# Hashed attention and a feed-forward block: the second feed-forward product as seven block products, in a remade order

## The chip, the cores and the metric

The kernel runs on one core of a Trainium2 chip. The metric is the device time of one execution in microseconds (us), the median of three runs. A core has five engines that run at the same time and meet only at semaphores: TensorE (PE, matrix products, with weight loads shown as PEld), VectorE (DVE), ScalarE (ACT), GpSimd (POOL) and SyncE (SP, which here issues transfers). Matrix products land in PSUM, which has eight banks of 512 f32 numbers for each of 128 partitions.

## The reference, cut to what matters

```python
# q, k, v: (4, 8, 768, 64); proj: (64, 6); w_ch1: (512, 2048); w_ch2: (2048, 512)
mask = bucket(q @ proj)[..., :, None] == bucket(k @ proj)[..., None, :]    # bucket: the signs as bits
scores = where(mask, q @ k.T / 8, -1e9)
x = softmax(scores) @ v               # then heads side by side: (4, 768, 512)
xn = (x - mean(x)) / sqrt(var(x) + 1e-6) * g_ln
out = x + maximum(xn @ w_ch1, 0.0) @ w_ch2
```

## The kernel before

The 4 x 768 rows are cut into twelve units `u` of 256 rows, three for each of the four batches. A unit goes through attention and then through the feed-forward block, and different units overlap.

Attention works on twice 4 heads (`g`) and on three blocks of 256 keys (`kp`), which makes 72 steps `s`. `S_` (L516) makes the scores: for each of 4 heads and two halves of the keys three matmuls of 256 columns, one of the hash bits (`G`) and two of the q and k halves. `E_` (L522) is the exponential on ScalarE, two instructions a step. `A_` (L541) multiplies by the values, with a column of ones for the sum. Then on VectorE `na` (L554) takes the accumulator out, `nb` (L561, L563) divides by the sum and writes `x`, `nc` (L567) and `ce` (L570, L571) make the statistics and the scaled rows `xc`, and `fl` turns them by a transfer into `xnT`. `rs` on GpSimd makes the reciprocal deviation, which is applied at the very end.

The feed-forward block of a unit: `F_` (L598) makes the first product, 16 blocks of 128 hidden columns for 256 rows, in eight parts `p` of two blocks; `R_` takes each part through max(., 0) into `hb`, on VectorE (L608) or ScalarE (L606). `hb` holds the hidden layer with the hidden column on the partition: 16 blocks `nt`, each 256 rows wide. `D_` (L614) makes the second product: for each half of the rows (`t`), 16 matmuls that sum over `nt`, each with 128 columns of `hb` as weights and 512 columns of `w2_sb` streamed, into one bank `f2`. `Z_` (L622) multiplies by the deviation and adds to `x`; `O_` sends `x` out. In unit 11 the second half of the rows is split into 384 and 128 columns.

Beside this, q and k of the next batch are loaded (`LX`), turned in 32 x 32 blocks on VectorE (`tu`, L270), cast to bf16 (`CA`) and hashed (`hm`, L471); v is cast on GpSimd (`cv`, L417) and summed over the keys there (`su`, L425 to L427). The first batch goes through shorter steps of its own (`lx`, `tn`, `ca`, `ha` at L359, `bh`).

The order is written out by hand or by a planner in the string `ORDER`: each word is a step, an engine letter (v, a, p, s, t) and its numbers, and the program issues the words one after the other. Each engine takes its own words in that order and waits only for the data and buffers it needs. `SLOTS` says which buffer each tile of a kind takes. PSUM is divided by name: `scA`, `scB` and `acc` are two banks each, `f1` and `f2` one each; F uses `f1` (and `f2` in unit 0), D uses `f2`.

Of the kernel before, what the change touches and what calls it, by code (L numbers as in the profile page):

```python
# [9 lines left out]
BF16 = mybir.dt.bfloat16  # L10
AOP = mybir.AluOpType
# [4 lines left out]
ROT = (0, 1, 2)  # L16


ORDER = """
mem.v lp.a lx.a.0.1.0.1 tab.a pf.v lx.s.0.0.0.1 warm.t wm.t.0 wm.t.1 wm.t.2 wm.t.3 sel.p  # L20
tn.v.0.0.0 p32.p tn.v.0.1.0 ca.p.0.1.0 lx.s.0.1.1.3 ha.t.0.0.0 wm.t.4 lx.s.1.1.0.3 lx.s.1.0.0.1 ha.t.0.1.0 lv.s.0.0.4 ca.a.0.0.0
lx.s.0.0.1.3 bh.v.0.0.0 wm.t.5 tn.v.0.1.1 ha.t.0.1.1 lw2.p.1 bh.v.0.1.0 ca.p.0.1.1 S.t.0.2 lv.s.0.4.4 E.a.0.0 E.a.0.1
tn.v.0.1.2 tn.v.1.1.1 ca.p.1.1.1 lx.s.1.0.1.3 wm.t.6 wm.t.7 bh.v.0.1.1 ha.t.1.1.1 on.p.0 bh.v.1.1.1 tn.v.1.1.0 S.t.1.2
E.a.1.0 ca.v.0.1.2 gx.p.1.0.0 ha.t.0.1.2 bh.v.0.1.2 E.a.1.1 tn.v.1.0.0 ca.p.1.0.0 ca.v.1.1.0 ha.t.1.1.0 bh.v.1.1.0 tn.v.1.1.2
S.t.2.2 E.a.2.0 cv.p.0.0.0 ha.t.1.0.0 bh.v.1.0.0 S.t.4.2 cv.p.0.0.2 tn.v.0.0.1 hc.t.0.0.1 ca.p.0.0.1 lw1.p.3 bc.v.0.0.1
gx.p.1.0.1 ha.t.1.1.2 LX.s.1.0.0 tn.v.0.0.2 E.a.2.1 E.a.4.0 LX.s.1.0.1 E.a.4.1 bh.v.1.1.2 sl.t.0.0.1 bi.v.0.0.1 cv.p.0.4.2
A.t.0.2 S.t.3.2 A.t.1.2 ca.v.1.1.2 lg.s lw1.p.1 sq.t.0.0 E.a.3.0 A.t.2.2 sc.v.0.0 E.a.3.1 S.t.5.2
E.a.5.0 cv.p.0.4.0 sq.t.0.4 na.v.0.0 nb.v.0.0 lw1.p.2 lw1.p.0 nc.v.0.0 E.a.5.1 S.t.8.2 sc.a.0.4 A.t.5.2
E.a.8.0 E.a.8.1 tu.v.1.0.0.2 lw2.p.0 tn.v.1.0.1 A.t.4.2 ca.p.1.0.1 hc.t.0.0.2 tn.v.1.0.2 A.t.3.2 tu.v.1.0.1.0 bc.v.0.0.2
lw2.p.3 gx.p.1.1.1 tu.v.1.0.0.1 sl.t.0.0.2 na.v.0.1 bi.a.0.0.2 S.t.6.2 E.a.6.0 LX.s.1.1.1 E.a.6.1 hc.t.1.0.1 nb.v.0.1  # L30
hc.t.1.0.2 bc.v.1.0.2 sl.t.1.0.2 bi.a.1.0.2 bc.v.1.0.1 pmem.p S.t.7.2 A.t.8.2 E.a.7.0 lv.s.1.4.1 nc.v.0.1 ce.v.0.1
ce.v.0.0 ft.t.0.1 lv.s.1.4.2 E.a.7.1 fc.a.0.1 sl.t.1.0.1 tu.v.1.0.1.1 bi.v.1.0.1 A.t.6.2 ft.t.0.0 S.t.9.2 E.a.9.0
on.p.1 lw2.p.2 fc.v.0.0 E.a.9.1 F.t.0.6 F.t.0.7 tu.v.1.0.1.2 R.a.0.6 A.t.7.2 tu.v.1.0.0.0 S.t.10.2 R.v.0.7
na.v.1.0 nb.v.1.0 lv.s.1.4.0 tu.v.1.0.0.3 tu.v.1.0.1.3 E.a.10.0 CA.p.1.0.1 F.t.0.3 F.t.0.4 E.a.10.1 A.t.9.2 ca.a.0.0.2
R.v.0.4 ca.a.1.0.2 S.t.11.2 gx.p.1.1.0 LX.s.1.1.0 E.a.11.0 E.a.11.1 lv.s.1.0.0 hm.t.1.0 R.v.0.3 F.t.0.5 S.t.14.2
R.a.0.5 A.t.11.2 A.t.10.2 E.a.14.0 E.a.14.1 bt.v.1.0 na.v.1.1 nb.v.1.1 F.t.0.2 R.a.0.2 S.t.12.2 nc.v.1.0
E.a.12.1 E.a.12.0 lv.s.1.0.1 F.t.0.0 R.v.0.0 mw.s.1.0 F.t.0.1 R.a.0.1 CA.p.1.0.0 tu.v.1.1.1.0 A.t.14.2 nc.v.1.1
ce.v.1.0 S.t.13.2 E.a.13.0 D.t.0.0.0 lv.s.1.0.3 tu.v.1.1.1.2 lv.s.1.4.3 D.t.0.0.1 fl.s.1.0 tu.v.1.1.0.2 ce.v.1.1 fl.s.1.1
tu.v.1.1.0.0 A.t.12.2 E.a.13.1 LX.s.2.0.0 S.t.16.2 E.a.16.0 E.a.16.1 A.t.13.2 tu.v.1.1.1.3 tu.v.1.1.0.1 tu.v.1.1.0.3 rs.p.0
D.t.0.0.2 D.t.0.0.3 mr.s.1.0.1 cv.p.1.4.0 Z.v.0.0 tu.v.1.1.1.1 CA.p.1.1.1 cv.p.1.4.2 S.t.15.2 lv.s.1.0.2 cv.p.1.0.0 E.a.15.0  # L40
mr.s.1.0.2 mr.s.1.0.3 hm.t.1.1 E.a.15.1 D.t.0.1.0 CA.a.1.1.0 S.t.17.2 E.a.17.1 mr.s.1.0.0 bt.v.1.1 mw.s.1.1 mr.s.1.1.3
na.v.2.0 nb.v.2.0 F.t.1.2 R.v.1.2 su.p.1.0 A.t.15.2 E.a.17.0 cv.p.1.0.2 A.t.16.2 F.t.1.6 S.t.18.2 R.a.1.6
nc.v.2.0 F.t.1.5 R.v.1.5 D.t.0.1.1 mr.s.1.1.2 E.a.18.0 A.t.17.2 E.a.18.1 sp.t.1.0 sc.v.1.0 na.v.2.1 S.t.20.2
E.a.20.0 mr.s.1.1.0 lv.s.2.4.1 F.t.1.0 tu.v.2.0.0.0 R.v.1.0 D.t.0.1.2 F.t.1.4 nb.v.2.1 nc.v.2.1 E.a.20.1 tu.v.2.0.0.3
R.a.1.4 S.t.19.2 E.a.19.0 E.a.19.1 D.t.0.1.3 ce.v.2.0 F.t.1.1 LX.s.2.0.1 su.p.1.4 rs.p.1 R.a.1.1 mr.s.1.1.1
Z.v.0.1 lv.s.2.0.1 lv.s.2.4.3 O.s.0.1 tu.v.2.0.1.2 lv.s.2.0.2 A.t.20.2 tu.v.2.0.1.1 S.t.21.2 ce.v.2.1 E.a.21.0 fl.s.2.0
F.t.1.3 D.t.1.0.0 E.a.21.1 A.t.18.2 rs.p.2 S.t.22.2 R.v.1.3 tu.v.2.0.0.1 tu.v.2.0.0.2 CA.v.2.0.0 A.t.19.2 fl.s.2.1
F.t.1.7 na.v.3.0 tu.v.2.0.1.3 O.s.0.2 R.v.1.7 E.a.22.0 E.a.22.1 D.t.1.0.1 S.t.23.2 F.t.2.1 lv.s.2.4.0 D.t.1.0.2
R.v.2.1 LX.s.3.1.0 nb.v.3.0 E.a.23.0 A.t.22.2 E.a.23.1 lv.s.2.0.0 F.t.2.0 LX.s.2.1.1 D.t.1.0.3 R.a.2.0 tu.v.2.0.1.0
CA.p.2.0.1 hm.t.2.0 S.t.24.2 E.a.24.1 Z.v.1.0 nc.v.3.0 bt.v.2.0 mw.s.2.0 sp.t.1.4 sc.v.1.4 A.t.21.2 lv.s.2.0.3  # L50
mr.s.2.0.2 D.t.1.1.0 A.t.23.2 O.s.0.0 E.a.24.0 na.v.3.1 O.s.0.3 tu.v.2.1.1.0 F.t.2.3 mr.s.2.0.3 cv.p.2.0.0 tu.v.2.1.1.1
R.a.2.3 nb.v.3.1 S.t.26.2 LX.s.2.1.0 D.t.1.1.1 E.a.26.0 E.a.26.1 nc.v.3.1 F.t.2.2 R.v.2.2 ce.v.3.1 D.t.1.1.2
mr.s.2.0.1 S.t.25.2 ce.v.3.0 F.t.2.4 LX.s.3.0.1 A.t.24.2 E.a.25.0 D.t.1.1.3 cv.p.2.0.2 R.v.2.4 S.t.29.2 E.a.25.1
tu.v.2.1.1.2 fl.s.3.1 Z.v.1.1 E.a.29.0 A.t.25.2 E.a.29.1 D.t.2.0.0 fl.s.3.0 F.t.2.7 R.a.2.7 S.t.28.2 A.t.26.2
tu.v.2.1.0.3 F.t.2.5 D.t.2.0.1 E.a.28.0 R.v.2.5 tu.v.2.1.0.1 E.a.28.1 na.v.4.0 S.t.31.2 E.a.31.1 tu.v.2.1.1.3 F.t.3.6
R.v.3.6 A.t.29.2 D.t.2.0.2 tu.v.2.1.0.2 tu.v.2.1.0.0 CA.v.2.1.0 E.a.31.0 F.t.2.6 R.a.2.6 O.s.1.3 S.t.27.2 E.a.27.0
D.t.2.0.3 nb.v.4.0 LX.s.3.0.0 O.s.1.2 hm.t.2.1 LX.s.3.1.1 nc.v.4.0 bt.v.2.1 mw.s.2.1 mr.s.2.1.3 Z.v.2.0 tu.v.3.0.0.2
E.a.27.1 tu.v.3.0.0.1 S.t.30.2 E.a.30.0 rs.p.3 su.p.2.0 F.t.3.4 A.t.27.2 R.a.3.4 on.p.2 D.t.2.1.0 D.t.2.1.1
E.a.30.1 F.t.3.1 R.v.3.1 S.t.32.2 CA.a.2.1.1 O.s.1.1 E.a.32.0 D.t.2.1.2 lv.s.3.0.0 F.t.3.2 tu.v.3.0.1.0 R.v.3.2
O.s.1.0 A.t.28.2 E.a.32.1 lv.s.2.4.2 S.t.35.2 E.a.35.0 E.a.35.1 na.v.4.1 F.t.3.0 cv.p.2.4.0 mr.s.2.0.0 D.t.2.1.3  # L60
Z.v.2.1 O.s.2.0 A.t.30.2 R.a.3.0 O.s.2.1 S.t.34.2 lv.s.3.0.2 mr.s.2.1.2 F.t.3.3 A.t.31.2 E.a.34.0 nb.v.4.1
R.v.3.3 tu.v.3.0.1.1 nc.v.4.1 ce.v.4.1 D.t.3.0.0 fl.s.4.1 ce.v.4.0 fl.s.4.0 E.a.34.1 tu.v.3.0.1.2 S.t.33.2 rs.p.4
D.t.3.0.1 A.t.32.2 E.a.33.0 tu.v.3.0.0.3 E.a.33.1 F.t.3.5 R.a.3.5 S.t.37.2 E.a.37.1 tu.v.3.0.0.0 cv.p.2.4.2 na.v.5.0
nb.v.5.0 D.t.3.0.2 A.t.33.2 F.t.3.7 A.t.35.2 E.a.37.0 R.v.3.7 nc.v.5.0 S.t.38.2 E.a.38.0 D.t.3.0.3 Z.v.3.0
mr.s.2.1.1 F.t.4.3 A.t.34.2 O.s.2.2 na.v.5.1 E.a.38.1 R.a.4.3 lv.s.3.0.3 O.s.2.3 tu.v.3.0.1.3 S.t.36.2 E.a.36.1
CA.v.3.0.1 F.t.4.0 R.a.4.0 nb.v.5.1 mr.s.2.1.0 CA.v.3.0.0 D.t.3.1.0 hm.t.3.0 bt.v.3.0 E.a.36.0 S.t.39.2 mw.s.3.0
E.a.39.0 F.t.4.2 A.t.38.2 R.a.4.2 tu.v.3.1.1.3 E.a.39.1 A.t.37.2 F.t.4.5 R.a.4.5 S.t.40.2 sp.t.2.0 sc.v.2.0
E.a.40.1 D.t.3.1.1 F.t.4.7 E.a.40.0 R.a.4.7 D.t.3.1.2 tu.v.3.1.0.0 S.t.41.2 E.a.41.0 F.t.4.4 R.a.4.4 A.t.36.2
mr.s.3.0.3 nc.v.5.1 ce.v.5.0 fl.s.5.0 ce.v.5.1 rs.p.5 na.v.6.0 su.p.2.4 fl.s.5.1 tu.v.3.1.1.0 D.t.3.1.3 Z.v.3.1
E.a.41.1 lv.s.3.0.1 F.t.4.1 R.v.4.1 S.t.44.2 E.a.44.0 E.a.44.1 A.t.41.2 D.t.4.0.0 F.t.5.2 S.t.43.2 E.a.43.0  # L70
tu.v.3.1.1.1 on.p.3 nb.v.6.0 A.t.40.2 nc.v.6.0 R.v.5.2 F.t.4.6 D.t.4.0.1 E.a.43.1 S.t.42.2 R.v.4.6 F.t.5.3
D.t.4.0.2 E.a.42.1 tu.v.3.1.0.2 cv.p.3.0.0 R.v.5.3 A.t.39.2 sp.t.2.4 E.a.42.0 O.s.3.3 sc.v.2.4 na.v.6.1 nb.v.6.1
S.t.45.2 E.a.45.1 E.a.45.0 lv.s.3.4.3 D.t.4.0.3 O.s.3.0 A.t.44.2 F.t.5.5 R.a.5.5 tu.v.3.1.1.2 A.t.43.2 S.t.47.2
E.a.47.0 Z.v.4.0 F.t.5.7 nc.v.6.1 ce.v.6.1 mr.s.3.0.1 O.s.3.1 E.a.47.1 fl.s.6.1 A.t.42.2 O.s.3.2 ce.v.6.0
na.v.7.0 D.t.4.1.0 S.t.46.2 E.a.46.0 D.t.4.1.1 lv.s.3.4.0 A.t.47.2 R.v.5.7 F.t.5.1 E.a.46.1 tu.v.3.1.0.1 A.t.45.2
# [605 lines left out]
```

## Time and profile before

| What | Value |
|---|---|
| Median of three runs | 305.0 us (304.3 to 305.05) |
| Span of the profiled execution, first to last instruction | 302.0 us |
| Mean granted TensorE clock | 1.000 |
| PE busy | 290.5 us (96%) |
| DVE busy | 175.9 us (58%) |
| ACT busy | 189.0 us (63%) |
| POOL busy | 76.4 us (25%) |
| Matmuls recorded, weight loads recorded | 4345, 4394 |

The time of the profiled execution itself is not listed apart from the runs; its span is 3.0 us under their median, and what is worked out on the span is carried over with these 3.0 us. The shares are means over the whole span. Each matmul has one weight load, so 49 records of matmuls are missing; they are all among those of L614 (351 of 400), and a group of L614 can therefore show fewer than its four matmuls. The end of a matmul in the records is modelled, so the time that one takes in a stream is read from start to start. In a group's row the last numbers are the idle time of its engine just before it and what ended that.

### The profile page before, as it was taken

What the parts mean: (1) busy time and instruction counts of PE and PEld (TensorE: products, weight loads), DVE (VectorE), ACT (ScalarE), POOL (GpSimd) and SP (SyncE); (2) the same over time, 40 slices, a digit from 0 to 9 for tenths busy, and PEclk for the clock granted to TensorE, in tenths of its full rate; (3) what the DMA queues carried; (4) which work ended last, traced back from release to release, by engine and by line L of the source; (5) the groups of instructions that cost most, each with busy time, mean ns of one, the idle gap of its engine ahead of it and who ended that gap; (6) DMA issues with size and microseconds to landing.
All of it is one profiled execution on the core that took longest, in us unless ns stands there. A gap on an engine that the chain in (4) does not pass through costs nothing.

```text
span 302.0 us, 9823 instructions
## 1 busy us (share of the span) xinstructions
PE 290.5 (96%) x4345; PEld 202.5 (67%) x4394; DVE 175.9 (58%) x364; ACT 189.0 (63%) x206; POOL 76.4 (25%) x103
## 2 busy tenths in 40 slices
PE   8988899999999999999999999999999999999995
PEld 4666677676766767677666776667666776676663
DVE  4878758759767564875749466274554346443322
ACT  2587888778646777777667866854565665643010
POOL 5497062476017101300750002700101001001000
PEclk9999999999999999999999999999999999999999
DMA  6999999718768453420322242012201501003132
GB/s 221 310 299 247 282 212 270 177 35 230 201 159 246 84 217 95 98 72 18 80 66 41 68 100 51 21 35 54 54 2 35 106 2 37 20 2 89 52 87 71
DMA packets 31194, 34.32 MB, mean 114 GB/s; under 512 B 15536, under 2 KB 27824, under 8 KB 31152
## 3 DMA queue, kind: packets, MB, share of 16 engines
q1 hardware_dynamic: 26080, 28.98, 35.0%
q0 software_dynamic: 4224, 4.19, 8.5%
q8 instruction: 34, 0.56, 0.8%
q10 hardware_dynamic: 848, 0.53, 0.7%
q14 instruction: 8, 0.07, 0.1%
HBM read 28.12 MB, written 6.88 MB: 116 GB/s over the span
## 4 chain that ended last, share of the span: by engine, by line
PE 94%; ACT 3%; issue 1%; DVE 0%
PE f L598 29%; PE sc L516 19%; PE acc L541 12%; PE hp L471 3%; ACT E L522 3%; PE hf L359 2%; PE warm L328 1%; PE f_110None L614 1%; PE f_101None L614 1%; PE f L614 1%; PE f_90None L614 1%; PE f_20None L614 1%; PE f_80None L614 1%; PE f_21None L614 1%; PE f_00None L614 1%
## 5 line engine op out<-in xcount | busy, mean ns | idle before, releaser
L522 ACT ACTIVATE E<-sc,bias_sb 128x1024 bf16<-128x1024 f32 x144 | 153.5, 1111 | 60.6 <-PE sc L516 60.6
L598 PE MATMUL f<-xnT,w_sb 128*128 128x256 bf16 x768 | 99.3, 273 | 0.1
L598 PEld LDWEIGHTS <-w_sb 128*128 128x128 bf16 x768 | 70.8, 98 | 22.6 <-issue 7.4
L608 DVE TENSOR_SCALAR hb<-f 128x512 bf16<-128x512 f32 x49 | 33.7, 690 | 59.2 <-PE f L598 58.8
L614 PEld LDWEIGHTS <-hb 128*128 128x128 bf16 x400 | 36.0, 98 | 31.2 <-issue 3.0
L516 PE MATMUL sc<-qb,kb 32*128 32x256 bf16 x1152 | 52.4, 267 | 0.0
L606 ACT ACTIVATE hb<-f 128x512 bf16<-128x512 f32 x47 | 28.0, 596 | 35.9 <-PE f L598 35.9
L541 PEld LDWEIGHTS <-E 128*128 128x128 bf16 x1152 | 42.7, 98 | 8.2 <-issue 3.2
L541 PE MATMUL acc<-vaug,E 128*128 128x65 bf16 x1152 | 46.2, 194 | 0.1
L516 PE MATMUL sc<-G 6*128 6x256 bf16 (+1 forms) x576 | 42.6, 273 | 2.7 <-ACT E L522 2.0
L576 POOL TENSOR_SCALAR rs<-mv 128x2 f32<-128x2 f32 x12 | 7.7, 640 | 106.9 <-DVE mv L570 106.6
L516 PEld LDWEIGHTS <-kb 32*128 32x128 bf16 x1152 | 30.4, 93 | 1.5
L516 PEld LDWEIGHTS <-G 6*128 6x128 bf16 (+1 forms) x576 | 15.7, 91 | 20.7 <-issue 17.4
L417 POOL CAST vaug<-vn 128x768 bf16<-128x768 f32 x16 | 14.0, 884 | 58.3 <-DMA vn<-in_v_dram 44.2
L270 DVE STREAM_TRANSPOSE T<-X 128x384 f32<-128x384 f32 (+2 forms) x52 | 26.8, 542 | 1.2 <-DMA X<-in_k_dram 1.2
L554 DVE SCALAR_TENSOR_TENSOR y<-vsB,acc 128x520 f32<-128x520 f32 x24 | 16.5, 688 | 10.5 <-PE acc L541 10.2
L571 DVE SCALAR_TENSOR_TENSOR xc<-x,mv,gB 128x512 bf16<-128x512 f32 x24 | 18.6, 775 | 0.9
L567 DVE BATCH_NORM_STATS2 st<-x 128x6 f32<-128x256 f32 x48 | 17.7, 412 | 0.3
L563 DVE TENSOR_TENSOR x<-y,rc 128x512 f32<-128x512 f32 x24 | 16.8, 699 | 0.8
L425 POOL TENSOR_TENSOR t<-vn 128x768 f32<-128x768 f32 x6 | 10.9, 1812 | 0.0
L281 POOL CAST kb<-T 128x1536 bf16<-128x1536 f32 x3 | 4.4, 1461 | 22.3 <-DVE T L270 22.3
L270 DVE STREAM_TRANSPOSE tp<-X 128x256 f32<-128x256 f32 x24 | 9.0, 416 | 1.4 <-DMA X<-in_q_dram 0.9
(113 smaller groups left out, 236.7 us busy)
## 6 DMA issues: line engine op xcount, KB each, us to landing
out_dram<-x SPq DMA_DIRECT2D x45, 128.0 KB, 2.0
X<-in_k_dram SPq DMA_DIRECT2D x7, 768.0 KB, 5.8
X<-in_q_dram SPq DMA_DIRECT2D x6, 768.0 KB, 4.7
vn<-in_v_dram SPq DMA_DIRECT2D x24, 192.0 KB, 6.0
w_sb<-in_moe_w_ch_dram POOLq DMA_DIRECT2D x8, 512.0 KB, 15.9
vn<-in_v_dram SPq DMA_DIRECT2D x2, 768.0 KB
X<-in_q_dram SPq DMA_DIRECT2D x2, 512.0 KB, 12.2
Bd<-B SPq DMA_DIRECT2D x6, 96.0 KB, 2.5
```

Source lines behind the costliest of these rows:

```text
L270: nc.vector.transpose(d[:, j], s[:, j, kj0 : kj0 + n])
L516: nc.tensor.matmul(sc(s, i // 2)[:, i % 2, 256 * kk : 256 * kk + 256], lh, rh, start=(rep == 0), stop=(rep == 2), skip_group_check=True,)
L522: nc.scalar.activation(E(s)[:, heads(h)], sc(s, h), AF.Exp, scale=EXP_SCALE, bias=bias_sb)
L541: nc.tensor.matmul(acc[:, qt, (D + 1) * i : (D + 1) * (i + 1)], E(s)[:, i, 256 * kk + P * qt : 256 * kk + P * qt + P], vaug(u // 3)[:, 4 * ...
L554: nc.vector.scalar_tensor_tensor(yt(u, g), vs, EPS_ROW, made[f"acc{u}{g}"][:, :, :A], op0=AOP.mult, op1=AOP.add,)
L563: nc.vector.tensor_tensor(xo, a[:, :, :, 0:D], rc.to_broadcast([P, 2, 4, D]), op=AOP.mult)
L567: nc.vector.bn_stats(stats(u)[:, qt, g], xt(u)[:, qt, 256 * g : 256 * g + 256])
L571: nc.vector.scalar_tensor_tensor(xc(u)[:, t], xt(u)[:, t], mv(u)[:, t, 0:1], gB, op0=AOP.subtract, op1=AOP.mult,)
L598: nc.tensor.matmul(f1[:, n].rearrange("p (t x) -> p t x", t=2), w1_sb[:, dt, P * nt : P * nt + P], xnT(u)[:, :, dt], start=(dt == 0), stop ...
L606: nc.scalar.activation(hb(u)[:, 2 * p : 2 * p + 2], f1, AF.Relu)
L608: eng.tensor_scalar_max(hb(u)[:, 2 * p : 2 * p + 2], f1, 0.0)
L614: nc.tensor.matmul(f2, hb(u)[:, nt, P * t : P * t + P], w2_sb[:, nt, half(h)], start=(nt == 0), stop=(nt == NNT - 1),)
```

## The change

Units 1 to 11 get another second product. The hidden layer of a unit and the second weight matrix are each cut into 2 x 2 blocks, A (rows by hidden columns) and B (hidden columns by output columns), and the product is made of seven block products instead of eight, in Winograd's form:

```
S1 = A21 + A22   S2 = S1 - A11   S3 = A11 - A21   S4 = A12 - S2
T1 = B12 - B11   T2 = T3 + B11   T3 = B22 - B12   T4 = B21 - T2
P1 = A11 B11   P2 = A12 B21   P3 = S4 B22   P4 = A22 T4   P5 = S1 T1   P6 = S2 T2   P7 = S3 T3
C11 = P1 + P2    C12 = P1 + P6 + P5 + P3
C21 = P1 + P6 + P7 + P4    C22 = P1 + P6 + P7 + P5
```

A block product `P` is 8 matmuls of 256 columns. P1, P6, P7 and P4 are added up in one accumulator X, which `Y` reads after each of them; P5 and P3 share one, Yb; P2 has its own. Each `Y` adds a partial sum into a quarter of `x` (128 rows, 256 columns). The four sums of weights are made once, in eight `sw` (half of them on GpSimd); the four sums of a unit, `ss`, are each one instruction over 128 x 1024 bf16, 25 of them on VectorE and 19 on GpSimd, and S3 takes the place of A21 in `hb`. Of the R steps 64 are on ScalarE and 32 on VectorE (47 and 49 before). Unit 0 keeps `D_` and `Z_`. PSUM tiles are dealt from two pools, three pairs of banks `pp` (scores, accumulators of attention) and two banks `f` (all the rest: F, P, D and the hash products), as the strings in `SLOTS` say. `ORDER` and `SLOTS` are remade from beginning to end. In the last stretch F, R, `ss`, `P` and `Y` of unit 11 stand behind each other with no scores left.

```diff
 ORDER (the end of it)
-D.t.11.1.0.0 D.t.11.1.1.0 D.t.11.1.2.0 O.s.8.2 D.t.11.1.3.0 D.t.11.1.0.1 D.t.11.1.1.1 rs.p.11 Z.v.11.0 O.a.11.0.0 O.s.11.0.1 Z.v.11.1.0
...
+R.a.10.3 F.t.10.5 F.t.10.4 O.s.9.3 R.a.10.5 F.t.10.0 R.a.10.4 P.t.10.2 Y.v.10.2 R.a.10.0
+F.t.11.4 ss.v.10.1 O.s.9.2 ss.v.10.2 R.a.11.4 P.t.10.1 Y.v.10.1 ss.v.10.4 P.t.10.5 P.t.10.6
+Y.v.10.5 P.t.10.3 Y.v.10.6 ss.p.10.3 Y.v.10.3 P.t.10.7 Y.v.10.7 F.t.11.0 R.a.11.0 P.t.10.4
...
+F.t.11.3 R.a.11.3 F.t.11.5 R.a.11.5 F.t.11.2 O.s.10.0 R.a.11.2 ss.v.11.1 ss.p.11.3 P.t.11.2
+Y.v.11.2 P.t.11.1 ss.v.11.2 O.s.9.1 Y.v.11.1 ss.v.11.4 P.t.11.5 Y.v.11.5 O.s.10.1 P.t.11.6
+Y.v.11.6 P.t.11.3 Y.v.11.3 O.s.10.2 O.s.11.0.0 O.a.11.0.1 P.t.11.7 Y.v.11.7 O.s.11.1.0.1 Y.v.11.7.1.0
+P.t.11.4 O.a.11.1.1.1 Y.v.11.4 O.a.11.1.1.0 O.s.11.1.0.0
...
+    wt = {n: pool.tile([P, 8, 256], BF16, name=f"wt{n}") for n in (2, 3, 4)}
...
     def ps(name, shape, tag, dt=F32):
         if name not in made:
-            made[name] = psum.tile(shape, dt, name=name, tag=tag)
+            n = taken.get(tag, 0)
+            taken[tag] = n + 1
+            made[name] = psum.tile(shape, dt, name=name, tag=f"{tag}_{SLOTS[tag][n]}")
...
-    def D_(eng, u, t, qtr, h=None):
...
+    def Hq(u, t, kh):
+        return hb(u)[:, 8 * kh : 8 * kh + 8, P * t : P * t + P]
+
+    def Wq(kh, h):
+        return w2_sb[:, 8 * kh : 8 * kh + 8, 256 * h : 256 * h + 256]
+
+    def Ss(u, k):
+        return Hq(u, 1, 0) if k == 3 else sb(f"S{u}{k}", [P, 8, P], BF16, "tp", 3)
...
+    def ss(eng, u, k):
+        out, in0, in1, op = {
+            1: (1, Hq(u, 1, 0), Hq(u, 1, 1), AOP.add),
+            2: (2, None, Hq(u, 0, 0), AOP.subtract),
+            3: (3, Hq(u, 0, 0), Hq(u, 1, 0), AOP.subtract),
+            4: (4, Hq(u, 0, 1), None, AOP.subtract),
+        }[k]
+        in0 = Ss(u, 1) if in0 is None else in0
+        in1 = Ss(u, 2) if in1 is None else in1
+        eng.tensor_tensor(Ss(u, out), in0, in1, op=op)
+
+    def prod(u, k):
+        if k in (1, 6, 7) or (k == 4 and u < NU - 1):
+            return "X"
+        return {2: "Ya", 5: "Yb", 3: "Yb", 4: "Yc"}[k]
+
+    def P_(eng, u, k):
+        left = {1: Hq(u, 0, 0), 2: Hq(u, 0, 1), 4: Hq(u, 1, 1)}
+        lh = left[k] if k in left else Ss(u, {3: 4, 5: 1, 6: 2, 7: 3}[k])
+        rh = {1: Wq(0, 0), 2: Wq(1, 0), 3: Wq(1, 1), 4: wt[4], 5: Wq(0, 1), 6: wt[2], 7: wt[3]}[k]
+        name = f"{prod(u, k)}{u}"
+        first = name not in made
+        f2 = ps(name, [P, 256], "f")
+        for n in range(8):
+            nc.tensor.matmul(f2, lh[:, n], rh[:, n], start=(first and n == 0), stop=(n == 7), skip_group_check=True)
+
+    def Y_(eng, u, k, *more):
+        t, h = more or {1: (0, 0), 2: (0, 0), 3: (0, 1), 4: (1, 0), 5: (1, 1), 6: (0, 1), 7: (1, 1)}[k]
+        x = xt(u)[:, t, 256 * h : 256 * h + 256]
+        nc.vector.scalar_tensor_tensor(
+            x, made[f"{prod(u, k)}{u}"], rstd(u)[:, t : t + 1], x, op0=AOP.mult, op1=AOP.add,
+        )
```

In the changed file `P_` is at L692, `Y_` at L697, `ss` at L677, `R_` at L634 and L636, `F_` at L626.

## The prediction

> **What bounds the kernel now.** The page comes first: its busy times, and the chain that ended last.
>
> ```profile
> span 302.0 us, 9823 instructions
> PE 290.5 (96%) x4345; PEld 202.5 (67%) x4394; DVE 175.9 (58%) x364; ACT 189.0 (63%) x206; POOL 76.4 (25%) x103
> PE 94%; ACT 3%; issue 1%; DVE 0%
> ```
>
> A busy PE need not be a full one, so the second view is the waits of PE alone, longest first:
>
> ```profile
> PE sc L516 <- ACT E L522: 2.0, 4, 0.7
> PE warm L328 <- DVE bias_sb L286: 1.1, 1, 1.1
> PE sc L516 <- DVE G L273: 0.6, 1, 0.6
> PE hf L383 <- DVE Bc L273: 0.5, 1, 0.5
> ```
>
> All of these lie in the first 35 us. After that TensorE has no wait for another engine over 0.1 us: each microsecond of matmul taken out is a microsecond off the span, if nothing new makes TensorE wait. The third view is the timeline of PE near the end, where only feed-forward products are left; it prices a matmul of each width:
>
> ```profile
> 286.66 1.04 PE L598 MATMUL f<-xnT,w_sb 128*128 128x256 bf16 x8
> 287.53 1.03 PE L614 MATMUL f_101None<-w_sb,hb 128*128 128x512 bf16 x4
> 288.39 1.04 PE L598 MATMUL f<-xnT,w_sb 128*128 128x256 bf16 x8
> ```
>
> From start to start, 8 matmuls of 256 columns take 0.87 us (109 ns each) and 4 of 512 take 0.86 (216 ns). So columns set the price, the fixed part is some 2 ns, and a weight load before each narrow matmul is hidden, since L598 has that already.
>
> **What the change saves.** A unit's second product was 32 matmuls of 512 columns: 32 x 0.216 = 6.91 us. Seven block products of 8 matmuls of 256 are 56 x 0.109 = 6.10. Ten units at 0.81 and unit 11 (its split halves summed 0.05 more) give 9.0 us. Unit 0 keeps D. The first score step also stands behind one hash product (L359) fewer, which took 0.96 us before it started at 9.13 us: I take 0.9, with 0 to 1.5 as its bounds, since ScalarE's exps follow closely there. Without new waits the span is 302.0 - 9.0 - 0.9 = 292.1.
>
> The Trainium skill, page "TensorE: Matmul & The Clock Gate", section "Back-to-back issue gap", speaks against the change: it gives 131 ns a matmul for a sustained stream with 512 columns and 81 with 128. By an estimate half-way between, 98 ns for 256, a unit would go from 4.2 to 5.5 us. The trace disagrees (216 and 109 ns).
>
> **What it costs the other engines.** Z at L622 took 0.75, 0.62 and 0.35 us for 512, 384 and 128 columns, so a Y of 256 takes 0.48 by a straight line. Out go the 20 Z of units 1 to 10 and the three of unit 11 (16.7 us), in come 78 Y (37.7). 17 R move from VectorE to ScalarE (-11.7, and +10.1 there). Sums: 29 on VectorE, 23 on GpSimd. No row shows a tensor_tensor all in bf16. L563 takes 0.70 for 512 f32; L591 shows 512 bf16 in the time (423 ns) that L447 needs for 256 f32 (424), so bf16 goes at double rate, and 1024 bf16 cost about 0.70. At L563's own rate they would cost 1.23; I take 0.70. Casts and copies that move to VectorE add 4.2, so it comes to 175.9 - 16.7 + 37.7 - 11.7 + 20.3 + 4.2 = 210 us (225 at 1.23). On GpSimd L425 (768 elements, 1.81 us) and L426 (256, 0.73) give 2.12 ns an element: a sum costs 2.35 us; bounds 1.1 (L417's one-input rate) and 2.7 (the dear L279 cast, 4.08 for 1536). 23 sums and three casts bring it to some 134 us. ScalarE stays at 190, since casts leave it as R comes. None is a bound over the whole span, but counted along ORDER from S.18 to S.42 VectorE has 77 us queued (83 at 1.23) against TensorE's 91, and from S.30 to S.36 it has 23 (25) against 24.
>
> **What makes TensorE wait.** Six of the seven products share two accumulators: P6 may start when Y1 has read bank X, P7 when Y6 has, P4 when Y7 has, P3 when Y5 has; P5, P6, P7, P3 need sums. VectorE takes its queue in order, so each Y stands behind the sums. And there is a contention in the trace of before. Three timelines, of VectorE and GpSimd together and then of each alone:
>
> ```profile
> 180.77 0.82 POOL L417 CAST vaug<-vn 128x768 bf16<-128x768 f32 x1 [25.36 <-DMA vn<-in_v_dram]
> 180.81 1.32 DVE L571 SCALAR_TENSOR_TENSOR xc<-x,mv,gB 128x512 bf16<-128x512 f32 x1
> ```
> ```profile
> 69.12 0.85 DVE L563 TENSOR_TENSOR x<-y,rc 128x512 f32<-128x512 f32 x1
> ```
> ```profile
> 68.70 0.72 POOL L426 TENSOR_TENSOR t<-t 128x256 f32<-128x256 f32 x1
> 69.50 1.06 POOL L427 TENSOR_TENSOR vsum<-t 128x256 bf16<-128x256 f32 x1
> ```
>
> L571 (two tensors from SBUF) takes 0.75 us elsewhere; started just behind a GpSimd cast it took 1.32, that is until the cast was done and its own work after. L563 waited for L426 and then L427 for L563. So a VectorE instruction with two SBUF inputs and a GpSimd one that reads exclude each other for their whole length. Y and na, with one input in PSUM, are free of it: L622 kept its 0.75 beside L425. The Trainium skill, "SBUF — State Buffer", section "Who interferes with whom", says the same of two SBUF inputs, and that whoever issues first gets the ports. By it too, the sums split over both engines block each other; the trace agrees (1.32 us against 0.75).
>
> I walk units through their queues with these prices (a reader of PSUM starts 0.22 us after the matmuls' slot; 0.1 us for a semaphore).
>
> Unit 11, from the end of F.11.2 as zero: R ends 0.8, first sum 0.9 to 1.6, Y2 to 2.1, P2 and P1 and P5 run to 2.6. The second sum would end at 2.8, Y1 at 3.3, so P6 starts 3.4, P3 at 4.6, P4 ends 7.2: 1.1 over the 6.1 of pure work. But ss.p.11.3 is released by the same first sum, while VectorE is in Y2: GpSimd holds the port from 1.7 to 4.05, the second sum ends at 4.6, and all after it is 1.8 later.
>
> Unit 10: both sums run first on VectorE, ss.p.10.3 then holds the port from 3.05 to 5.4, and the third sum waits from 3.55; Y5 and Y6 stand behind it, P3 starts at 6.5 instead of 4.8. By order alone 0.4, by the port 1.7.
>
> Unit 8: as unit 11, with Y2 between the sums: 1.0 and 1.8. Unit 7: ce.8.0 comes while ss.p.7.2 runs, Y1 and so P6 are 1.0 late, over 0.5 by order alone. Unit 6: third sum behind ss.p.6.2, covered by S, F: 0.3 and 0. Unit 9: both GpSimd sums run while VectorE has only Y's: 0 and 0.
>
> Units 6 to 11 lose 3.3 by order and 6.3 by the port. Units 1 to 5 I did not walk; scores and F lie between their products as in 6 and 7, so I give each those units' mean, 0.4 and 0.5: 2.0 and 2.5. In unit 2, ss.p.2.4 and ss.v.2.3 with nb.4.1 behind it meet, so it may be more. Total: 5.3 by order, 8.8 by the port. If the sums cost 1.23, each unit's chain of two to three is up to 1 us longer (some 4 more where not covered); with GpSimd sums at 1.1 the port costs 4 instead of 8.8. The order alone has as bounds 2.5 (half, where engines run ahead) and 8.
>
> Sum: 292.1 + 5.3 + 8.8 = 306.2 of span. The median of the runs, 305.0, lies 3.0 above the profiled span of 302.0, and I add the same: 309.
>
> **Rivals.** (1) The port is not met on the path: the order places the GpSimd sums where VectorE is in Y's, transposes or R's, as it does in unit 9. For it: 7 such meetings in the trace of before, over 41 GpSimd reads, and none made TensorE wait. Against: in units 7, 8, 10 and 11 the same instruction releases both sides. It gives 292.1 + 5.3 + 3.0 = 300.4 us, faster. The change wins as soon as the port costs less than 3.7, two of the four meetings. Chance 0.40 for this side.
> (2) VectorE becomes the bound in units 2 to 5: its 77 us of 91 grow by five or six blocked instructions of up to 2.35, so Y's and R's run late throughout and F waits for its two banks too. For it: its queue is over 80% full there; against: R left it. It adds 3 to 5 to the forecast: 312 to 314. Chance 0.10.
> (3) Matmuls are paid by the piece: if a narrow matmul cost over 124 ns (6.91/56), the products would save nothing. The rows give 109 and the fixed part 2 ns. At 130 ns, 56 x 21 ns x 11 = 13 us more than the sum: 322. Chance 0.02. This is what the skill's rule on the gap would amount to; the trace speaks against it.
> That the products are not there is no rival: the instruction list has 616 matmuls of 256 columns where 368 stood.
>
> **Numbers.** About 0.3%, 0.9 us, is what a measurement of this kernel can tell from no change. Forecast (order and port) 0.41, own range 306 to 314; VectorE bound 0.10; by the piece 0.02; port not met 0.40, own range 297.5 to 303.5; in between, 304.1 to 305.9, 0.07. So faster 0.40, same 0.07, slower 0.53. The range goes from 298 (rival 1 with the order's waits at half, 2.5: 292.1 + 2.5 + 3.0 = 297.6) to 314; some 0.08 is left out below it and 0.10 above.
>
> **What would show it.** Right: Matmul groups of the products at 109 ns; PE's waits, new, on VectorE's Y (L697) and sums (L677), 10 us or more together, most in units 7, 8, 10, 11; VectorE's sums of 0.70 that last 2 to 3 us whenever a GpSimd sum runs; PE busy under 285. Wrong: sums on both engines overlapping at full speed, or PE waits under 6 us in total, which would give a time under 302; or idle PE before E or F, which would put the cost elsewhere.

## The result and the profile after

The changed kernel takes 318.6 us (median of four runs, 315.9 to 320.4) against 304.7 us for the kernel before: a ratio of 1.046, with an interval of 1.040 to 1.051. It is 14 us slower; the forecast was 309, with 314 as the upper end. Ratios leave out executions that took over 1.5% more than the fastest of the same kernel (five of ten in run 6, at most a third in any other); in runs 6, 13 and 16 the ratio is therefore given and not the median.

The profiled execution took 318.7 us, 1.7 more than its span. Its page, first the length, the busy times and the chain that ended last:

```profile
span 317.0 us, 10500 instructions
...
PE 290.3 (92%) x4642; PEld 228.3 (72%) x4642; DVE 228.2 (72%) x438; ACT 190.5 (60%) x213; POOL 131.8 (42%) x129
...
PE 54%; DVE 18%; DMA 13%; issue 5%; SPq 3%; POOL 3%; ACT 3%; DVEq 0%; POOLq 0%
```

The chain had been 94% PE. Now 18% of it is VectorE and 13% transfers, where the kernel before had next to nothing of either. The waits of PE, longest in total first (us in total, times, longest):

```profile
PE X L692 <- DVE x L697: 6.0, 6, 1.7
PE Yb L692 <- DVE x L697: 3.7, 4, 2.2
PE f L626 <- DMA w_sb<-in_moe_w_ch_dram: 2.8, 1, 2.8
PE sc L544 <- DMA G<-Bd: 1.6, 1, 1.6
PE f L641 <- DVE B L302: 1.3, 1, 1.3
```

The first two rows, 9.7 us, are the new waits of products on Y that were forecast. Their place was not: 5.4 of them lie in units 1 to 3, 0.3 in unit 4, and 4.0 in units 7, 8, 10 and 11, where most were expected. The next two rows are a weight transfer and the hash bits, which the prediction did not have. All gaps of PE come to 21.1 us, against 6.6 before.

The products themselves cost what was said. The timeline of PE near the end:

```profile
309.70 1.03 PE L692 MATMUL Yb<-w_sb,S 128*128 128x256 bf16 x8
310.57 1.04 PE L692 MATMUL X<-wt,hb 128*128 128x256 bf16 x8
311.44 1.04 PE L692 MATMUL Yc<-wt,hb 128*128 128x256 bf16 x8
```

A group of eight starts every 0.87 us, 109 ns a matmul. And the meeting of the two engines in unit 11 came as walked. VectorE's timeline, then GpSimd's:

```profile
304.82 0.69 DVE L677 TENSOR_TENSOR S<-hb 128x1024 bf16<-128x1024 bf16 x1 [5.38 <-ACT hb L634]
305.43 0.48 DVE L697 SCALAR_TENSOR_TENSOR x<-Ya,rs,x 128x256 f32<-128x256 f32 x1
305.82 2.43 DVE L677 TENSOR_TENSOR S<-S,hb 128x1024 bf16<-128x1024 bf16 x1
```
```profile
305.59 2.12 POOL L677 TENSOR_TENSOR hb<-hb 128x1024 bf16<-128x1024 bf16 x1 [10.90 <-DVE S L677]
```

The second sum takes 2.43 us in place of 0.69: it holds until GpSimd is done at 307.71 and then does its own work. Over the whole run VectorE's instructions last some 25 us longer than the shortest of the same line and shape (some 2 before; differences over 0.15 us counted).

**Where the time went.** From the start of a unit's first score step (step 6`u` of the 72) I take off the TensorE work that the order puts ahead of it (each word at its price in the trace of before: a score step some 0.8, a group of F or of a product 0.87, and so on). What is left is lag: waits, slow clock and a late start. In us, from the profiled executions:

| Lag at | before | after |
|---|---|---|
| start of unit 3 | 8.7 | 13.4 |
| start of unit 6 (products of 1, 2 and half of 3 lie behind it) | 9.5 | 25.2 |
| start of unit 9 (of 3 to 5 too) | 10.1 | 26.4 |
| start of unit 11 (of 6 and 7 too) | 10.5 | 27.6 |
| last matmul | 11.2 | 34.5 |

23.3 us of lag are new, and 9.1 us of work are gone: 14.2, as the last matmul ends 14.2 later (312.5 against 298.3). Of the new lag 15.7 us lie ahead of unit 6, where the prediction had 1.4 (two and a half units at 0.9, less 0.9 at the start).

A view that explains much of the early part is the waits of VectorE on the q and k of the next batch, in the changed kernel and then before:

```profile
DVE T L299 <- DMA X<-in_k_dram: 3.8, 2, 3.1
DVE T L299 <- DMA X<-in_q_dram: 3.7, 1, 3.7
```
```profile
DVE T L270 <- DMA X<-in_k_dram: 1.2, 1, 1.2
```

VectorE stands still for 7.5 us, until 65.7, 80.1 and 117.2 us, because they are not there to be turned, and its queue (R, Y, sums) stands behind. Why they are late shows on SyncE's own timeline ("SPq" rows are issues of transfers):

```profile
87.48 0.86 SPq L443 DMA_DIRECT2D vn<-in_v_dram  x2
99.83 0.34 SPq L518 DMA_DIRECT2D Bd<-B  x1
...
112.14 0.36 SPq L482 DMA_DIRECT2D X<-in_k_dram  x1
```
```profile
117.17 0.58 DVE L299 STREAM_TRANSPOSE T<-X 128x384 f32<-128x384 f32 x1 [3.08 <-DMA X<-in_k_dram]
```

From 88.4 to 99.8 us the queue waits for hash bits to write (`mw`, L518). The input that VectorE needs at 114 is behind it and is issued at 112.1, though its buffer had been free since 88.3.

TensorE's own waits ahead of unit 6 fit the new lag: behind the start, eight of over 0.9 us come to 12.2 us, and two windows of half clock (last section) to up to 3.4 more. Late transfers are not alone in them. Ahead of three of the four waits for Y there (at 92.6, 123.1 and 144.6 us) stands a VectorE instruction that a GpSimd one held up, a division and two sums that take 0.69 us undisturbed:

```profile
89.95 2.21 DVE L591 TENSOR_TENSOR x<-y,rc 128x512 f32<-128x512 f32 x1
...
119.11 2.26 DVE L677 TENSOR_TENSOR hb<-hb 128x1024 bf16<-128x1024 bf16 x1
...
140.76 2.65 DVE L677 TENSOR_TENSOR S<-S,hb 128x1024 bf16<-128x1024 bf16 x1
```

The second is the meeting in unit 2 (`ss.p.2.4` with `ss.v.2.3`) of which the prediction said that it may cost more.

### The profile page after: what moved, and what is told of

Same layout as the page of the kernel before. It is cut to its first block, busy times and chain, and to the rows that moved or that the text cites. A ratio compares the mean times of both kernels' runs of the same rounds, so it can differ in the third digit from the quotient of the medians.

```text
span 317.0 us, 10500 instructions
## 1 busy us (share of the span) xinstructions
PE 290.3 (92%) x4642; PEld 228.3 (72%) x4642; DVE 228.2 (72%) x438; ACT 190.5 (60%) x213; POOL 131.8 (42%) x129
## 4 chain that ended last, share of the span: by engine, by line
PE 54%; DVE 18%; DMA 13%; issue 5%; SPq 3%; POOL 3%; ACT 3%; DVEq 0%; POOLq 0%
PE f L626 21%; PE sc L544 9%; PE X L692 8%; PE acc L569 6%; DMA w_sb<-in_moe_w_ch_dram 5%; PE Yb L692 4%; DMA vn<-in_v_dram 3%; DVE S L677 3%; DVE T L299 3%; DVE x L697 3%; DMA X<-in_q_dram 3%; DVE x L591 2%; PE hp L500 2%; PE Ya L692 2%; ACT E L550 2%
## 5 line engine op out<-in xcount | busy, mean ns | idle before, releaser
L626 PE MATMUL f<-xnT,w_sb 128*128 128x256 bf16 x768 | 97.0, 277 | 5.4 <-DMA w_sb<-in_moe_w_ch_dram 2.8
L626 PEld LDWEIGHTS <-w_sb 128*128 128x128 bf16 x768 | 72.9, 99 | 18.7 <-issue 7.1
L634 ACT ACTIVATE hb<-f 128x512 bf16<-128x512 f32 x64 | 38.0, 597 | 49.0 <-PE f L626 46.0
L692 PEld LDWEIGHTS <-hb 128*128 128x128 bf16 x352 | 33.0, 98 | 7.2 <-issue 3.2
L677 POOL TENSOR_TENSOR hb<-hb 128x1024 bf16<-128x1024 bf16 x8 | 17.9, 2233 | 47.9 <-DVE S L677 47.9
L636 DVE TENSOR_SCALAR hb<-f 128x512 bf16<-128x512 f32 x32 | 21.9, 686 | 19.3 <-PE f L626 18.9
L692 PEld LDWEIGHTS <-S 128*128 128x128 bf16 x264 | 25.2, 97 | 14.7 <-issue 8.1
L697 DVE SCALAR_TENSOR_TENSOR x<-X,rs,x 128x256 f32<-128x256 f32 x44 | 20.8, 476 | 11.9 <-PE X L692 11.3
L692 PE MATMUL Yb<-w_sb,S 128*128 128x256 bf16 x176 | 22.8, 272 | 3.7 <-DVE x L697 3.7
L446 POOL CAST vaug<-vn 128x768 bf16<-128x768 f32 x16 | 14.2, 902 | 26.6 <-DMA vn<-in_v_dram 26.6
L591 DVE TENSOR_TENSOR x<-y,rc 128x512 f32<-128x512 f32 x24 | 23.8, 992 | 0.8
L599 DVE SCALAR_TENSOR_TENSOR xc<-x,mv,gB 128x512 bf16<-128x512 f32 x24 | 22.6, 942 | 0.8
L692 PE MATMUL X<-wt,hb 128*128 128x256 bf16 x168 | 21.8, 273 | 0.7 <-DVE x L697 0.7
L677 POOL TENSOR_TENSOR S<-S,hb 128x1024 bf16<-128x1024 bf16 x5 | 10.6, 2123 | 27.3 <-DVE S L677 27.2
(90 smaller groups left out, 315.4 us busy)
```

The source lines that it names most:

```text
L591: nc.vector.tensor_tensor(xo, a[:, :, :, 0:D], rc.to_broadcast([P, 2, 4, D]), op=AOP.mult)
L599: nc.vector.scalar_tensor_tensor(xc(u)[:, t], xt(u)[:, t], mv(u)[:, t, 0:1], gB, op0=AOP.subtract, op1=AOP.mult,)
L626: nc.tensor.matmul(f1[:, n].rearrange("p (t x) -> p t x", t=2), w1_sb[:, dt, P * nt : P * nt + P], xnT(u)[:, :, dt], start=(dt == 0), stop ...
L634: nc.scalar.activation(hb(u)[:, 2 * p : 2 * p + 2], f1, AF.Relu)
L636: eng.tensor_scalar_max(hb(u)[:, 2 * p : 2 * p + 2], f1, 0.0)
L677: eng.tensor_tensor(Ss(u, out), in0, in1, op=op)
```

## The experiments

Sixteen kernels, in the order in which they ran. Their line numbers lie 5 to 14 below those of the changed kernel; tile names are the same. All are edits of the changed kernel's order (words of `ORDER`), with buffers dealt out again where that asks for it. Run 4 also adds a scratch instruction, runs 5 and 11 bring back the plain product, and in runs 6, 7, 12 and 13 the products read plain blocks in place of the sums left out. Medians stand beside a kernel before of 304.0 to 304.9, and where runs of different groups are compared that counts for up to 1 us.

**1. All sums on VectorE.**

```diff
-ss.p.1.3 ss.p.2.2 ... sw.p.3.0 ...
+ss.v.1.3 ss.v.2.2 ... sw.v.3.0 ...      (19 ss and 4 sw)
```

> All 19 sums of hidden blocks and the 4 sums of weight blocks that the changed kernel leaves to GpSimd run on VectorE, at the same places of the order. Theory (the port: a VectorE operation that reads two SBUF blocks and a GpSimd operation hold each other up): VectorE takes 23 x 0.69 = 16 us more work and loses 21 of the 25 us by which its instructions are prolonged now, so its busy time stays near 223 to 228; no sum lasts over 1 us; the waits of the products on Y and on sums fall from 9.7 us to under 4; 308 to 312 us. Rival (the order: VectorE's queue is the limit, and who adds is no matter): the 16 us of added work stand in front of Y, 319 to 324 us. Rival (early weight wait and clock): no change, 317 to 320 us.

Measured: 315.4 us, ratio 1.035 [1.033, 1.038], 3.2 below the changed kernel; the expectation was 308 to 312 or no gain. The same group of sums in the changed kernel and here (busy us, mean ns of one, idle before them):

```profile
L677 DVE TENSOR_TENSOR S<-S,hb 128x1024 bf16<-128x1024 bf16 x6 | 11.0, 1829 | 0.3
```
```profile
L670 DVE TENSOR_TENSOR S<-S,hb 128x1024 bf16<-128x1024 bf16 x11 | 7.6, 691 | 0.2
```

One takes 691 ns in place of 1829, and what VectorE loses in all falls from some 25 to some 7 us, as the port theory says. But 16 us of added sums take most of it back: products now wait 4.7 us for Y and 6.3 for sums, where under 4 in all was expected.

**2. Two weight transfers issued early.**

```diff
+lw1.p.2 behind lw1.p.3, lw1.p.0 behind cv.p.0.4.2 (some 100 words earlier)
```

> Only the issues of two weight transfers (the W1 columns of F.0.5 and those that follow) go back to an earlier place of GpSimd's queue, about where the kernel before has them. If the wait of 2.80 us at 40.4 us and the half clock that follows it for one window of 3.41 us are a cost of their own: both go, 4.5 us less, 313 to 315 us. If the wait was slack that is found again later (VectorE the limit in units 0 to 2): no change, 317 to 320 us. The port theory says nothing of it, beyond that this is a separate part of the loss.

Measured: 317.4 us, 1.043 [1.038, 1.048], not told apart from the changed kernel. The 2.8 us wait is gone, but PE waits 2.2 us at 78 us for R, behind VectorE's wait for an input, and the clock is at half after it. A miss: what was won was mostly spent again at VectorE's wait.

**3. Three late sums on VectorE.**

```diff
-ss.p.8.3 ss.p.10.3 ss.p.11.3
+ss.v.8.3 ss.v.10.3 ss.v.11.3
```

> Three sums only (block 3 of units 8, 10 and 11) move from GpSimd to VectorE: the three whose GpSimd partner, by the trace of after, kept a VectorE sum for 1.84, 2.64 and 2.43 us in place of 0.69. Port theory: each of the three partners takes 0.7 again and the third sum stands 0.7 behind them; units 8, 10 and 11 give back 0.5 to 1.7 us each, 314.5 to 317 us. Order rival: VectorE has 0.7 us more ahead of each Y, no gain or 1 to 2 us more, 318 to 321 us.

Measured: 317.0 us, 1.042 [1.039, 1.045]; the median is just inside what the port theory gave, but the intervals overlap. The lag behind the start of unit 11 tells more: 4.0 us, where it was 6.9.

**4. As 1, with scratch sums on GpSimd.**

```diff
+dm.p... behind each of the 23 moved words: tensor_tensor of the same size into a scratch tile
```

> As with all sums on VectorE, but behind each of the 23 moved sums GpSimd also makes one of the same size from the same or like blocks into a scratch tile that nobody reads. No product waits for GpSimd any more; what is left of GpSimd's part is only its hold on the port. Port theory: VectorE's operations are prolonged again by 15 us or more, on top of 16 us of added work, and 6 to 12 us of time come back: 316 to 324 us. Rival (what hurt was the 2.1 us latency of a GpSimd sum in front of a product): same time as without the scratch sums, within 1 us.

Measured: 336.4 us, 1.105 [1.100, 1.109]: 21 us above run 1, more than either theory gave. VectorE loses some 30 us again. One meeting, VectorE's timeline and GpSimd's:

```profile
240.20 2.64 DVE L672 TENSOR_TENSOR S<-S,hb 128x1024 bf16<-128x1024 bf16 x1
```
```profile
240.17 2.12 POOL L681 TENSOR_TENSOR dm<-S,hb 128x1024 bf16<-128x1024 bf16 x1 [11.10 <-DVE S L672]
```

GpSimd began 0.03 us earlier, and VectorE's sum took 2.64 us. In the trace nothing waits for a scratch sum, so it is not a sum's latency that hurts here; of the two theories the port is left. (GpSimd's casts of v also stand behind the scratch sums, as they stand behind the real ones in the changed kernel; and five of the 22 windows of half clock told of below fall in this run. So 21 us is more than the port alone.)

**5. Plain products in the remade order.**

```diff
-P.t.1.2 Y.v.1.2 P.t.1.1 Y.v.1.1 P.t.1.5 ...
+D.t.1.0.2 D.t.1.0.3 D.t.1.0.0 ... Z.v.1.0 ...  (no ss, no sw; banks dealt out again)
```

> The changed kernel's order, pools and early stages, but units 1 to 11 make the plain product: eight groups of four matmuls of 512 columns stand at the seven places of the block products (two groups at the last), two full-width Z at the ends take the place of the seven Y, and all sums, of hidden blocks and of weights, are gone; the PSUM banks of the pool are dealt out again for that. If the remade order and the pool by themselves cost little: TensorE has the 9 us back and the sums' and Y's 37 us are off VectorE, 303 to 307 us, as the kernel before; the loss of after is then the sums' and Y's. If the remade order is itself the loss (early weights, hash bits, buffers): 312 to 320 us.

Measured: 318.9 us, 1.046 [1.043, 1.049]. The order without any sums is as slow, which pointed away from the sums. It does not show what the order alone costs, though: a plain product holds a bank through 16 matmuls, where the order counts on one being free for F again. That is a likely reason and was not tried by itself.

**6 and 7. No sums; no GpSimd sums.**

```diff
-ss.v... ss.p...      (6: all 44;  7: the 19 ss.p)
```

> All 44 sums of hidden blocks are left out (the products read plain hidden blocks in their place; the 8 instructions on the weights stay); the products, the Y and the order are those of after. Theory (VectorE with its port is what the sums fill): 17 us off VectorE, 40 us off GpSimd, and with them all waits on Y over 1 us behind a sum; what is left is the early wait for weights, the hash bits and one or two half-clock windows: 303 to 308 us. If the seven Y and the order are what holds: 311 to 316 us.

> Only the 19 sums on GpSimd are left out (the products, and the sums that would read them, read plain hidden blocks instead); VectorE's 25 sums stay. By the port theory this takes away most of the 21 us by which VectorE's instructions are prolonged, and adds nothing to VectorE: 307 to 312 us, so 3 to 8 us below the run with all sums on VectorE (315.4). If GpSimd's sums hurt nothing but through VectorE's added 16 us in that run, it stays at 314 to 317 us.

Measured: 1.000 [0.997, 1.004], so some 305 us, for run 6, and 307.8 us, 1.010 [1.008, 1.012], for run 7. All sums together cost 14 us in this order, and GpSimd's 19 cost 11 of these; VectorE's 25 cost 3. Both in the range of the port theory. But without any sums the 9 us of the products are still not there: in both runs VectorE waits for inputs (6.8 us in the trace of run 7; 10 in that of run 6, whose profiled execution took 308.7 us).

**8 and 9. Three inputs early; the weights too.**

```diff
+LX.s.2.0.1 ahead of mw.s.1.0;  LX.s.2.0.0 behind fl.s.1.0;  LX.s.2.1.1 ahead of mw.s.2.0
+9: lw1.p.2 and lw1.p.0 as in run 2
```

> Three input transfers only move in SyncE's queue: the one of 60.7 us to ahead of the write of the first hash bits, behind which that queue stood from 29.9 to 50.1 us; the one of 72.0 us to behind the transpose issued at 58.7; the one of 112.1 us to ahead of the third write of hash bits, behind which the queue stood from 88.4 to 99.8 us. New theory (late inputs stop VectorE's queue): VectorE's three waits on X of 0.7, 3.7 and 3.1 us go, with them TensorE's waits of 80 to 93 and of 117 to 123 us and one half-clock window, 6 to 9 us less: 310 to 313 us. If VectorE only idles there and has the same work late anyway: 316 to 319 us.

> The three inputs early and the two weight transfers early as well. If both early transfers stand ahead of the same VectorE queue, the 2.8 us and its half-clock window, which alone were worth 1.2 us, now count in full: 4 us below the run with early inputs alone, 306 to 309 us. If not, 1 us below it.

Measured: 312.6 us, 1.029 [1.025, 1.032], and 310.9 us, 1.023 [1.019, 1.027]. SyncE's timeline of run 8:

```profile
83.48 0.85 SPq L436 DMA_DIRECT2D vn<-in_v_dram  x2
84.43 0.37 SPq L475 DMA_DIRECT2D X<-in_k_dram  x1
96.31 0.34 SPq L511 DMA_DIRECT2D Bd<-B  x1
```

The input of 112.1 us goes out at 84.4, ahead of the hash bits. VectorE has no wait for an input left, and neither half-clock window of the changed kernel comes. That is 6.0 us for three moved words by the medians (5.2 by the ratios), at the lower end of what was expected, and 1.7 for the weights, less than the 4 expected: in run 8 the wait for weights is down to 1.5 us and no slow clock follows it. The lag at the start of unit 6 falls from 25.2 to 19.2 and then 16.9.

**10. Early transfers, sums of units 1 to 5 and the three late ones on VectorE.**

```diff
+as 9; ss.v and sw.v for all of units 1 to 5; ss.v.8.3 ss.v.10.3 ss.v.11.3
```

> As the run before, and the sums of units 1 to 5 and of the weights all on VectorE, and three late sums (block 3 of units 8, 10, 11) too: by the two earlier runs the first is worth 6 us up to the start of unit 6, the second 3 us behind it. Port theory: 4 to 8 us below the run with early transfers alone, 299 to 304 us, and so at or below the kernel before. If VectorE fills up instead: 305 to 310 us.

Measured: 310.9 us, 1.022 [1.019, 1.025], no gain, a miss for the port theory as put. The lag shows two parts: 4.6 us less at the start of unit 6 (12.3 against 16.9), and 6.3 more between the starts of units 8 and 9, where unit 5's sums stand in VectorE's queue.

**11. Plain products with early transfers.** Edit of run 5 with those of run 9.

> Plain products in the remade order (which took 318.9 us), with the three inputs and the two weight transfers early. If the late transfers are what the remade order costs, 306 to 310 us, near the kernel before; if it is the pool of PSUM banks or something else of the order, 314 to 319 us.

Measured: 320.8 us, 1.053 [1.048, 1.059]: no gain. So with plain products it is not the transfers that hold; this run and run 5 say nothing on the order beyond that it fits only the products it was made for.

**12 and 13. Early transfers, no sums; no GpSimd sums.** Edits of runs 6 and 7 with those of run 9.

> Transfers early as in the run of 310.9 us, and all 44 sums of hidden blocks left out (plain hidden blocks in their place). If the product term of the prediction holds (-9.0 us of TensorE time that nothing else takes back) and the early order costs 1 to 3 us more than before's: 296 to 299 us. If the seven Y or the pool cost as much as the products gain: 302 to 306 us.

> Transfers early and only the 19 sums on GpSimd left out. Port theory, with the prediction's price: 8 to 10 us below the run with all sums (310.9), 300 to 303 us, and 2 to 4 us above the run without any. If GpSimd's sums by now hurt only at the last three units: 306 to 308 us.

Measured: 300.2 us, 0.984 [0.980, 0.989], and 0.999 [0.996, 1.003], so some 304.4 us. The products gain 4.5 us when nothing has to be added up, less than expected (296 to 299), and run 13 is a miss too (300 to 303). All sums cost 11 to 12 us in the early-transfer order (10.7 by the medians, 11.8 by the ratios), GpSimd's 19 some 7 of them.

**14. As 10, with unit 5's three sums back on GpSimd.**

```diff
-ss.v.5.2 ss.v.5.3 ss.v.5.4
+ss.p.5.2 ss.p.5.3 ss.p.5.4
```

> Transfers early; sums of units 1 to 4 and of the weights on VectorE, unit 5's three as in the changed kernel on GpSimd, and the three late sums on VectorE. In the run with unit 5 on VectorE too, units 1 to 4 gave back 4.6 us up to the start of unit 6, and unit 5's sums, seven in 15 us of VectorE's queue behind two long divisions, lost 6.3 us again between units 8 and 9. If that reading is right: 302 to 306 us, about the kernel before. If VectorE's queue is full whichever unit's sums it takes: 309 to 312 us.

Measured: 305.2 us, 1.001 [0.997, 1.004], as the reading of run 10 said: the kernel before is reached, not beaten. Its page:

```profile
span 303.7 us, 10496 instructions
...
PE 289.3 (95%) x4639; PEld 228.3 (75%) x4642; DVE 220.8 (73%) x452; ACT 190.3 (63%) x213; POOL 102.5 (34%) x115
```

All gaps of PE are 8.9 us here (21.1 in the changed kernel, 6.6 before). The longest is for hash bits, 1.45 us at 63.1 us.

**15 and 16. The second early input behind the reads of hash bits; and one sum of unit 4 back on GpSimd.**

```diff
+15: LX.s.2.0.0 ahead of mw.s.1.1        16: also ss.p.4.3
```

> As the run of 305.2 us, with the second early input one place group later in SyncE's queue, behind the reads of the first hash bits. If the wait of 1.45 us and its half-clock window (1.7) are that input's doing: 302 to 304 us, 0.3 to 1 percent under the kernel before. If the wait is the hash bits' own chain: 304.5 to 306 us.

> As the last, and block 3 of unit 4 back on GpSimd, as in the changed kernel. If the 0.87 us wait at 137.2 us is VectorE reaching that sum late: another 0.5 to 1 us, 301.5 to 303.5 us. If the sum's 2.1 us on GpSimd stands in its place: no change or 1 us more.

Measured: 307.1 us, 1.008 [1.005, 1.011], and 1.006 [1.002, 1.009], so some 306.2 us. Run 15 is slower than run 14, run 16 is not told apart from either: two misses. In run 15 TensorE waits longer, and at 72.7 us, for hash bits:

```profile
PE sc L537 <- DMA G<-Bd: 2.5, 1, 2.5
```

And in run 16 the 0.87 us wait stays (0.86). It was taken for one of unit 4, but the product that waits is P7 of unit 3, for unit 3's third sum on VectorE; run 16 moved a sum that stands behind it.

## Why the prediction was wrong

It had the direction (slower, with 0.53) and missed the size: 318.6 against 309. Step by step, with the lag of the trace beside each term:

- **Products, -9.0.** The price per matmul held (109 ns; the prediction's other value, 98, lies a third of the way from 81 to 131 and not half-way, and did not come). In time, without sums and with early transfers, 4.5 us are there (run 12); the prediction's products, startup and order terms together gave -4.6. That the two agree is luck: the order term is in part for sums, which run 12 leaves out, and it was put mostly late, while the lag of run 12 lies mostly early (15.6 us at the start of unit 6, 9.5 before).
- **Startup, -0.9.** TensorE's first score step started 0.16 us earlier. Mis-sized, within its bounds.
- **Prices.** Y took 482 ns (0.48 said), a sum on VectorE 690 where nothing disturbed it (0.70), on GpSimd 2120 (2.35). VectorE's busy time is 228 and not 210: what its instructions lose while held up, some 25 us, counts as busy and was not added to the sum; without it some 203 would be left.
- **The walk of units 6 to 11, 3.3 by order and 6.3 by the port.** The new lag there is 7.0 us (the rows from unit 9 to the end, 8.1, less 1.1 before). Unit 11 went as walked. In unit 10 GpSimd's third sum met the second sum of VectorE (2.64 us) and not the third. Sound, a little dear.
- **From the middle of unit 3 to unit 5, not walked, 2.3.** The new lag is 0.6.
- **The failed step: units 1 to 3, everything ahead of unit 6.** The prediction did not walk units 1 to 3. It gave them the mean of later units, 0.9 each, and the startup -0.9, and it never walked the queues that issue transfers, though SyncE's order was remade like the others: late transfers stood in the sum at nothing. There lie 15.7 us of new lag in place of 1.4. Runs 8 and 9 give back 8.3 of them (and 7.7 us of time by the medians, 6.9 by the ratios) by moving five issues of transfers alone: inputs that stood behind `mw`, and weights far down GpSimd's queue. Moving sums of units 1 to 4 then gives back another 2.6 (run 14; 4.6 in run 10). The remaining 4.8 are not shown in full; in run 14 a wait for hash bits (1.45) with its half-clock window (up to 1.7) is among them. These shares hold for this order of repairs: with the transfers left late, all sums on VectorE (run 1) or GpSimd's 19 left out (run 7) take 6.5 and 6.2 us off the same lag. So late transfers and the port in units 1 to 3 are both shown, and how the 15.7 divide between them stays open. In time: without sums, the prediction's own terms leave at most 300 us (292.1 + 5.3 + 3.0), and run 6 took some 305.
- **From span to time, +3.0.** Executions of both kernels list 1.7 us between span and time, so by its span the profiled execution of before took 1.3 us less than the median. These 1.3 us in the sum were chance, and brought the forecast nearer.

With 14.3 more lag ahead of unit 6 than said, 1.7 less up to unit 9, 2.6 less behind, and 0.75 more between the last matmul and the end of the span, 306.2 becomes 317.0.

Of the rivals, "port not met" is refuted by runs 1, 4 and 7. "VectorE the bound in units 2 to 5" had the place right, but not the size (312 to 314 us) nor the whole cause: held-up instructions cost VectorE 8 us between the starts of units 3 and 6, as it said, but in the same stretch VectorE also stood still for 6.8 us, waiting for inputs. "By the piece" is refuted by the 109 ns.

Of the signs named beforehand, products at 109 ns, waits on Y of some 10 us, and sums of 2 to 3 us beside a GpSimd sum came. That most of the waits lie in units 7, 8, 10 and 11 did not (4.0 of 9.7 us). Nor did PE busy under 285 (290.3): two half-clock windows lie in it, and ahead of each of some 20 waits the last matmul counts as busy 0.16 us beyond its slot (recorded as 272 ns, with starts 109 apart). And the sign of being wrong, idle PE before F, came: 2.8 us for weights.

## What to carry to other kernels

When a whole order is remade, walk every queue, those that only issue transfers too: a transfer that stands behind a write waiting for its data is late however free its buffer is, and here three such words cost 5 to 6 us. Sums that an algorithm adds have a price per place, not per piece: the same 44 sums cost 14 us with the transfers late, 11 to 12 with them early, and 5 once each was on the engine that its place allows. And an engine pair that shares a port is to be walked as one engine wherever both read.

## What the runs showed of the hardware

In these traces TensorE's clock is granted in windows of 3.41 us on a fixed grid, and a window through which TensorE idles for well over half is followed by one at half speed. In the changed kernel, stretches on that grid (length; then busy us of PE, PEld, DVE, ACT and POOL; the clock; DMA share; GB/s):

```profile
36.48:39.89 3.41, 1.10 (x36) 0.76 (x27) 1.84 (x4) 2.13 (x3) 0.00 (x0) 1.00 1.07 345
39.89:43.30 3.41, 2.92 (x14) 2.11 (x15) 0.99 (x2) 0.00 (x0) 0.00 (x0) 0.50 1.18 250
74.02:77.43 3.41, 1.76 (x32) 1.12 (x30) 2.31 (x3) 1.77 (x3) 3.11 (x4) 1.00 0.96 248
77.43:80.84 3.41, 3.41 (x45) 2.81 (x39) 0.75 (x3) 2.12 (x2) 2.81 (x2) 0.50 0.46 165
```

TensorE idles 68% and 48% of the first and third, and the second and fourth run at 0.50. Over the profiled executions of all 18 kernels, every window idle for over 54% was followed by a slow one, none under 42% was, and between these it went either way (one window of run 4 stayed slow though TensorE idled 11% of the one ahead). So a wait of 1.5 us can cost up to 1.7 more behind it, half of a window. In run 8 one of 1.5 us falls across two windows and has no slow one behind it; but in run 11 one of 1.7 us falls within one (49%) and has none either, so what decides between 42 and 54% is not shown. The Trainium skill, page "TensorE: Matmul & The Clock Gate", section "Why this matters for your kernels", asks for no idle gaps over some 3 us; here single gaps of 1.45 us (run 14) and 1.65 us (the changed kernel) were enough.

The port held up the later instruction in both directions. With a lead of 0.03 us for GpSimd, VectorE's sum of 0.69 us took 2.64 (run 4). Where a division of VectorE stood ahead, begun at 167.5 and 191.3 us of the changed kernel, GpSimd's next sum of 2.12 us took 2.57 and 2.58. The Trainium skill, page "SBUF — State Buffer", section "Who interferes with whom", says that whoever issues first has it for the whole instruction; the traces agree.
